# Second expert layer: slots of two and three full tiles, the rest of the first round moved into the second

## The chip, the cores and the metric

One core of one Trainium2 chip runs the whole program in one launch. The metric is device time in microseconds (us). The kernel before takes 890.9 us (median of 3 runs, 889.74 to 891.76).

## The reference

Three stages run after one another on 2304 tokens of 512 numbers, all in float32. Attention with random features (4 batches, 8 heads, 576 positions) makes `x`. A dense gated layer follows: `silu(x @ w_gate) * (x @ w_val) @ w_out` with 1536 hidden columns. Last comes a layer of 8 experts with 1024 hidden columns, in which each token goes to one expert:

```
logits = x @ w_gate + modality_bias[modality_id]
e_idx = np.argmax(logits, axis=1)
...
for e in range(E):
    mask = e_idx == e
    h = np.maximum(x[mask] @ w1[e], 0.0)
    out[mask] = gate_w[mask, None] * (h @ w2[e])
```

With the inputs of the reference only two experts are used: 1127 tokens go to expert 4 and 1177 to expert 5. Of the first 1920 tokens (15 tiles of 128) they get 934 and 986, of the last 384 tokens 193 and 191.

## The kernel before, in words

Products are made exact enough for float32 by splitting each operand into a high and a low part and adding three matmuls (`mm3`, L167 to L170). The 18 token tiles form 6 groups of 3 (`GT`). `moe1_group` (L912) runs the dense layer of a group: 12 blocks of hidden columns, each with 24 matmuls of 384 columns (into `gv`) and 9 of 512 (into `acc`). `finish` (L959) copies the three rows of results out, stores them to a scratch array in DRAM (`scr`), and schedules the logits: 24 dot products on VectorE (`logits_rows`, L735), then the softmax and the running rank of each token within its expert (`group_route`, L762).

The expert layer works in slots. A slot is 256 tokens of one expert: it loads that expert's weights (4 MB, 8 loads `raw`, L1027), splits them into 16 tiles `w` (`sp`, one copy on ScalarE and one subtraction on VectorE each, L173 and L174), gathers its token rows by an indirect DMA of GpSimd (`grow`, L1043), transposes them (`gx`, L1055; `sx`, L1057 and L1058), and runs for each of 8 blocks 12 matmuls of 256 columns (`h`) and 6 of 512 (`acc`). Between them ScalarE makes `uh` (L1094) and VectorE `ul` (L1095). The results are scaled (`orow`, L1116 and L1118) and scattered to `out` (L1120). There are two rounds: 8 slots for the first 15 tiles and 2 for the last 3. Further slots run only if a count on the chip asks for them (`more`). 

`finish_route` (L802) decides for each round, wholly on VectorE but for some small matmuls, which token goes to which slot. It is a list of pieces: `a` counts tokens, `b` builds comparisons of 15 or 3 tiles with all columns of all possible slots, then for three tiles at a time `f` makes three matrices `f_lh` and `g` multiplies with them on TensorE (`inv`, L887), and `d` reads indices out. The first round's pieces run during the last group of the dense layer, the second's during the slots.

The order on every engine is written out at build time (`manual_schedule`). `Tasks` keeps a list of pieces with due times in a planner's time: TensorE's work calls `T.step(dt)`, which first emits every piece that is due. So the planner's time fixes only the order in which each engine's queue gets its instructions; each engine then takes its own queue strictly in that order and waits by semaphores. `slot_prefetch` (L1012) places the next slot's loads, splits, gather and transposes in this way, `LQ` and `LS` the logits' dot products, `FO` and `FC` the pieces of `finish_route`:

```
fr = after + 6
T.at(T.now + fr + (FO * i if i < 2 else 2.6 * FO + FC * (i - 2)), f)
```

## Time and profile before

| | |
|---|---|
| profiled execution | 892.92 us, of which span 891.2 us |
| median of the runs | 890.9 us |
| TensorE matmul (PE) | 864.9 us busy, 97% |
| VectorE (DVE) | 616.8 us, 69% |
| ScalarE (ACT) | 390.4 us, 44% |
| GpSimd (POOL) | 92.5 us, 10% |
| mean granted TensorE clock | 0.992 of full |

The span runs from the first to the last instruction; 1.7 us of the execution lie around it. A busy share is a mean over stages with different limits: the dense layer's last group runs from about 564 to 643 us, the ten slots from there to 879 us. A matmul's listed duration overlaps the next one, so what one costs is the distance from its start to the next start.

### The profile page before, as it was taken

What the parts mean: (1) busy time and instruction counts of PE and PEld (TensorE: products, weight loads), DVE (VectorE), ACT (ScalarE), POOL (GpSimd) and SP (SyncE); (2) the same over time, 40 slices, a digit from 0 to 9 for tenths busy, and PEclk for the clock granted to TensorE, in tenths of its full rate; (3) what the DMA queues carried; (4) which work ended last, traced back from release to release, by engine and by line L of the source; (5) the groups of instructions that cost most, each with busy time, mean ns of one, the idle gap of its engine ahead of it and who ended that gap; (6) DMA issues with size and microseconds to landing.
All of it is one profiled execution on the core that took longest, in us unless ns stands there. A gap on an engine that the chain in (4) does not pass through costs nothing.

```text
span 891.2 us, 15112 instructions
## 1 busy us (share of the span) xinstructions
PE 864.9 (97%) x5320; PEld 798.7 (90%) x5320; DVE 616.8 (69%) x1565; ACT 390.4 (44%) x1071; POOL 92.5 (10%) x215
## 2 busy tenths in 40 slices
PE   7989899999999999999999999999999999999994
PEld 6879888999999999999999999999999999999993
DVE  5989899466665666566665665488777778866640
ACT  4865666343333343233344321212555555555530
POOL 6701211000000000000000000000211111111100
PEclk9989999999999999999999999999999999999998
DMA  8726542022222112131112111224497776677500
GB/s 263 209 65 202 177 162 78 8 76 54 65 54 72 36 43 54 42 95 42 42 37 60 37 26 35 57 73 175 133 337 246 245 247 228 199 233 220 174 18 22
DMA packets 91728, 103.44 MB, mean 116 GB/s; under 512 B 53600, under 2 KB 55666, under 8 KB 91643
## 3 DMA queue, kind: packets, MB, share of 16 engines
q1 hardware_dynamic: 88171, 92.35, 33.9%
q0 software_dynamic: 3200, 9.97, 3.2%
q8 instruction: 44, 0.72, 0.3%
q14 instruction: 41, 0.34, 0.1%
q10 hardware_dynamic: 272, 0.07, 0.0%
HBM read 92.91 MB, written 9.98 MB: 115 GB/s over the span
## 4 chain that ended last, share of the span: by engine, by line
PE 63%; issue 17%; DVE 7%; DMA 5%; POOL 4%; ACT 2%; POOLq 0%; DVEq 0%; ACTq 0%
PE gv L168 11%; PE gv L170 10%; PE gv L169 10%; PE acc L168 6%; PE acc L170 6%; PE acc L169 6%; DMA out_dram<-orow,sidx 5%; PE num L601 2%; PE kv L568 2%; POOL grow L1043 2%; PE qt L592 1%; PE pr L168 1%; PE xt L483 1%; PE pr L169 1%; PE pr L170 1%
## 5 line engine op out<-in xcount | busy, mean ns | idle before, releaser
L168 PE MATMUL gv<-xT,w 128*128 128x384 f32 x576 | 202.4, 351 | 1.1 <-DVE th L935 1.0
L170 PE MATMUL gv<-xT,w 128*128 128x384 f32 x576 | 194.5, 338 | 0.0
L169 PE MATMUL gv<-xT,w 128*128 128x384 f32 x576 | 194.4, 337 | 0.0
L168 PE MATMUL acc<-w,uh 128*128 128x512 f32 x360 | 146.7, 407 | 0.0
L169 PE MATMUL acc<-w,uh 128*128 128x512 f32 x360 | 141.8, 394 | 0.0
L170 PE MATMUL acc<-w,ul 128*128 128x512 f32 x360 | 141.4, 393 | 0.0
L546 ACT ACTIVATE h<-pr,mx 128x128 f32<-128x128 f32 x224 | 64.0, 369 | 138.9 <-DVE mx L541 127.3
L168 PEld LDWEIGHTS gv<-xT,w 128*128 128x128 f32 x576 | 108.9, 189 | 5.2 <-DVE th L935 2.4
L169 PEld LDWEIGHTS gv<-xT,w 128*128 128x128 f32 x576 | 109.1, 189 | 2.6
L174 DVE TENSOR_TENSOR w<-raw,w 128x512 fp32r<-128x512 f32 x160 | 106.6, 688 | 6.2 <-ACT w L173 2.4
L170 PEld LDWEIGHTS gv<-xT,w 128*128 128x128 f32 x576 | 108.7, 189 | 0.0
L747 DVE SCALAR_TENSOR_TENSOR wge<-xrow,wge 128x512 f32<-128x512 f32 x144 | 98.7, 685 | 10.1 <-DMA wge<-wg2t 9.5
L173 ACT CAST w<-raw 128x512 fp32r<-128x512 f32 x160 | 92.8, 617 | 4.3 <-DMA raw<-in_moe_w_dram 4.3
L168 PE MATMUL h<-sx,w 128*128 128x256 f32 x320 | 91.6, 286 | 0.0
L170 PE MATMUL h<-sx,w 128*128 128x256 f32 x320 | 90.5, 283 | 0.0
L169 PE MATMUL h<-sx,w 128*128 128x256 f32 x320 | 90.4, 283 | 0.0
L170 PEld LDWEIGHTS acc<-w,ul 128*128 128x128 f32 x360 | 67.6, 188 | 15.4 <-DVE ul L1095 0.2
L168 PEld LDWEIGHTS acc<-w,uh 128*128 128x128 f32 x360 | 68.0, 189 | 7.3
L169 PEld LDWEIGHTS acc<-w,uh 128*128 128x128 f32 x360 | 68.1, 189 | 7.0
L944 ACT CAST uh<-th 128x384 fp32r<-128x384 f32 x72 | 37.5, 521 | 66.2 <-DVE th L939 66.0
L935 DVE SCALAR_TENSOR_TENSOR th<-th,gv 128x384 f32<-128x384 f32 x72 | 39.7, 551 | 38.1 <-ACT th L932 38.0
L525 DVE TENSOR_REDUCE mx<-pr 128x4 f32<-128x512 f32 x72 | 49.5, 687 | 23.2 <-PE pr L170 19.7
(194 smaller groups left out, 1432.0 us busy)
## 6 DMA issues: line engine op xcount, KB each, us to landing
raw<-in_moe_w_dram SPq DMA_DIRECT2D x80, 512.0 KB, 4.8
wge<-wg2t SPq DMA_DIRECT2D x48, 256.0 KB, 3.4
wraw<-in_moe_w_gate_dram SPq DMA_DIRECT2D x12, 512.0 KB, 4.5
wraw<-in_moe_w_val_dram SPq DMA_DIRECT2D x12, 512.0 KB, 4.8
wraw<-in_moe_w_out_dram SPq DMA_DIRECT2D x12, 512.0 KB, 4.5
scr<-xrow SPq DMA_DIRECT2D x18, 256.0 KB, 2.3
xin<-in_q_dram SPq DMA_DIRECT2D x26, 128.0 KB, 2.3
xin<-in_k_dram SPq DMA_DIRECT2D x24, 128.0 KB, 2.7
```

The source lines that it names most:

```text
L168: nc.tensor.matmul(o, lh, rh, start=start, stop=False, skip_group_check=True)
L169: nc.tensor.matmul(o, lh, rl, start=False, stop=False, skip_group_check=True)
L170: nc.tensor.matmul(o, ll, rh, start=False, stop=stop, skip_group_check=True)
L173: nc.scalar.copy(hi, src)
L174: nc.vector.tensor_tensor(out=lo, in0=src, in1=hi.bitcast(F32), op=ALU.subtract)
L525: nc.vector.tensor_reduce(out=mx, in_=pr, axis=AX.X, op=ALU.max)
L546: nc.scalar.activation(out=h[:, a, :], in_=pr[:, a, :], func=ACTF.Exp, bias=mx[:, a:a + 1])
L568: nc.tensor.matmul(kv_ps[0][:, g, :], h[:, c, :], vt[:, c, 0:D + 1], start=t == own[0] and c == 0, stop=t == own[-1], skip_group_check=True)
L601: nc.tensor.matmul(num[r:r + m, h, :], st["h"][:, h, r:r + m], kv_sb[b, j][:, h, :], start=True, stop=True)
L747: nc.vector.scalar_tensor_tensor(out=st[e][:, 1, :], in0=xrows[i], scalar=1.0, in1=st[e][:, 0, :], op0=ALU.mult, op1=ALU.mult, accum_out=L ...
L935: nc.vector.scalar_tensor_tensor(out=th[f], in0=th[f], scalar=1.0, in1=ps.pop((f, "g")), op0=ALU.add, op1=ALU.mult)
L944: nc.scalar.copy(u[f][0], th[f])
```

## The change

Both rounds now count in tiles of 128 tokens. The first round takes of each expert only full tiles, in slots of two tiles (4 of them) and three tiles (2), and lowers the ranks and counts by what it took. The second round covers all 18 tiles: it holds the last three and whatever is left of the first 15, in one slot of three tiles and one of two (run in this order), and slots that run only on demand belong to it alone. So every row is stored to both scratch arrays, except the last three. `finish_route` is cut into more and smaller pieces: eight pieces `FO` apart, then the pairs `f`, `g`, where `f` now also builds its three slices of the multiplied matrix (`mv`, in the pool `rows`). The dot products of the last group come 8.5 instead of 10.37 apart, the last group's rows lie in the pool `w`, results in `rows`. A path of `wsteps` that is never taken (`n % 99 == 98` for n under 36) is gone. The core of the diff:

```diff
-LQ = (10.37, 4.52, 0.96)
+LQ = (8.5, 4.52, 0.96)
 LATE = 6
-FO = 5.72
+FO = 1.9
...
+        for g, n2, n3 in ((0, 4, 2), (1, 1, 1)):
             r = Round()
+            r.nt = (NTILE - GT, NTILE)[g]
+            r.n2, r.n3, r.fixed = n2, n3, 2 * n2 + 3 * n3
+            r.cap = g * ((NT - E) // (2 * P) + E)
+            r.C = r.fixed + 2 * r.cap
+            r.C += r.C % 2
+            r.slots = [(2, 2 * i, i) for i in range(n2)] + [(3, 2 * n2 + 3 * i, n2 + i) for i in range(n3)]
+            r.scr = dram.tile([r.nt * P, DM], F32, name=f"scr{g}")
+            r.cum = const.tile([P, E], F32, name=f"cum{g}")
             rounds.append(r)
+        nc.vector.memset(rounds[0].cum, 0.0)
...
+            return rounds[t >= rounds[0].nt]
...
+            A, B2 = rounds
+            second = r is B2
+            C, nt = r.C, r.nt
+            ts = slice(0, nt)
+            nsl = r.n2 + r.n3 + r.cap
...
+            def sums(x, k):
...
+                nc.vector.memset(s0[:, :, 0:E], 0.0)
+                nc.vector.memset(s1[:, :, 0:E], 0.0)
+                nc.vector.tensor_copy(s0[:, :, E:], x)
+                for a, b, n in ((s0, s1, 1), (s1, s0, 2), (s0, s1, 4)):
+                    nc.vector.tensor_tensor(out=b[:, :, E:], in0=a[:, :, E:], in1=a[:, :, E - n:2 * E - n], op=ALU.add)
+                return s1[:, :, E:]
+            def count():
...
+                nc.vector.tensor_tensor(out=cmp_, in0=bc(r.cum, 2, [P, E, n]),
+                                        in1=bc(THR[:, 0:n] if second else THR[:, 1:n + 1], 1, [P, E, n]),
+                                        op=ALU.is_gt if second else ALU.is_ge)
+                nc.vector.tensor_reduce(out=tl, in_=cmp_, axis=AX.X, op=ALU.add)
...
+                nc.vector.tensor_tensor(out=cmp_[:, :, 0:n], in0=bc(tl, 2, [P, E, n]),
+                                        in1=bc(cst["iota"][:, 2:2 * n + 1:2], 1, [P, E, n]), op=ALU.is_ge)
+                nc.vector.tensor_reduce(out=h, in_=cmp_[:, :, 0:n], axis=AX.X, op=ALU.add)
...
+                nc.vector.scalar_tensor_tensor(out=ab[:, 1, :], in0=h, scalar=-2.0, in1=tl, op0=ALU.mult, op1=ALU.add)
+                nc.vector.tensor_tensor(out=ab[:, 1, :], in0=ab[:, 1, :], in1=h, op=ALU.min)
+                nc.vector.tensor_tensor(out=ab[:, 0, :], in0=h, in1=ab[:, 1, :], op=ALU.subtract)
+            def place():
...
+                st["inc"] = inc = sums(ab, 2)
...
+                nc.vector.tensor_tensor(out=pre, in0=inc, in1=ab, op=ALU.subtract)
+                for i, n in enumerate((r.n2, r.n3)):
+                    nc.vector.tensor_scalar(out=got[:, i, :], in0=pre[:, i, :], scalar1=-1.0, scalar2=float(n),
+                                            op0=ALU.mult, op1=ALU.add)
+                nc.vector.scalar_tensor_tensor(out=got, in0=got, scalar=0.0, in1=ab, op0=ALU.max, op1=ALU.min)
...
+                nc.vector.tensor_tensor(out=done, in0=got[:, 0, :], in1=got[:, 1, :], op=ALU.add)
+                nc.vector.scalar_tensor_tensor(out=done, in0=done, scalar=2.0, in1=got[:, 1, :], op0=ALU.mult, op1=ALU.add)
+            def offsets():
...
+                if second:
...
+                    nc.vector.tensor_tensor(out=rest, in0=st["nt"], in1=done, op=ALU.subtract)
+                    nc.vector.tensor_tensor(out=cmp_, in0=bc(rest, 2, [P, E, n]),
+                                            in1=bc(cst["iota"][:, 1:2 * n:2], 1, [P, E, n]), op=ALU.is_ge)
+                    nc.vector.tensor_reduce(out=dn[:, 0, :], in_=cmp_, axis=AX.X, op=ALU.add)
+                    st["dinc"] = sums(dn, 1)
...
+                    nc.vector.tensor_tensor(out=offd, in0=st["dinc"][:, 0, :], in1=dn[:, 0, :], op=ALU.subtract)
+                    nc.vector.tensor_scalar(out=offd, in0=offd, scalar1=float(2 * P), scalar2=float(P * r.fixed),
+                                            op0=ALU.mult, op1=ALU.add)
+                nc.vector.tensor_scalar(out=done, in0=done, scalar1=float(P), scalar2=None, op0=ALU.mult)
...
+                nc.vector.tensor_scalar(out=lim2, in0=got[:, 0, :], scalar1=float(2 * P), scalar2=None, op0=ALU.mult)
+                nc.vector.tensor_scalar(out=off2, in0=pre[:, 0, :], scalar1=float(2 * P), scalar2=None, op0=ALU.mult)
+                nc.vector.tensor_scalar(out=off3, in0=pre[:, 1, :], scalar1=float(3 * P), scalar2=float(2 * P * r.n2),
+                                        op0=ALU.mult, op1=ALU.add)
+                nc.vector.tensor_tensor(out=off3, in0=off3, in1=lim2, op=ALU.subtract)
+                if second:
+                    nc.vector.tensor_tensor(out=offd, in0=offd, in1=done, op=ALU.subtract)
+                    nc.vector.tensor_tensor(out=offd, in0=offd, in1=off3, op=ALU.subtract)
+                nc.vector.tensor_tensor(out=off3, in0=off3, in1=off2, op=ALU.subtract)
+            def ranks():
...
+                nc.vector.tensor_tensor(out=y, in0=rk, in1=bc(st["lim2"], 1, sh), op=ALU.is_ge)
+                nc.vector.tensor_tensor(out=y, in0=y, in1=bc(st["off3"], 1, sh), op=ALU.mult)
+                nc.vector.tensor_tensor(out=x, in0=rk, in1=bc(st["off2"], 1, sh), op=ALU.add)
+                nc.vector.tensor_tensor(out=x, in0=x, in1=y, op=ALU.add)
+            def ranks2():
...
+                nc.vector.tensor_tensor(out=y, in0=rk, in1=bc(st["done"], 1, sh), op=ALU.is_ge)
+                if second:
+                    nc.vector.tensor_tensor(out=y, in0=y, in1=bc(st["offd"], 1, sh), op=ALU.mult)
+                    nc.vector.tensor_tensor(out=x, in0=x, in1=y, op=ALU.add)
+                    nc.vector.tensor_scalar(out=y, in0=rk, scalar1=0.0, scalar2=None, op0=ALU.is_lt)
+                nc.vector.scalar_tensor_tensor(out=x, in0=y, scalar=FAR, in1=x, op0=ALU.mult, op1=ALU.add)
+                nc.vector.tensor_tensor(out=x, in0=x, in1=OH[:, ts, :], op=ALU.mult)
...
+                nc.vector.tensor_reduce(out=dest, in_=x, axis=AX.X, op=ALU.add)
+                if not second:
+                    nc.vector.tensor_tensor(out=rk, in0=rk, in1=bc(st["done"], 1, sh), op=ALU.subtract)
+                    nc.vector.tensor_tensor(out=B2.cum, in0=r.cum, in1=st["done"], op=ALU.subtract)
+            def experts():
...
+                parts = [(st["inc"][:, 0, :], r.n2), (st["inc"][:, 1, :], r.n3)]
+                if second:
+                    parts.append((st["dinc"][:, 0, :], r.cap))
+                for inc, n in parts:
+                    nc.vector.tensor_tensor(out=se[:, at:at + n, :], in0=bc(inc, 1, [P, n, E]),
+                                            in1=bc(cst["iota"][:, 0:n], 2, [P, n, E]), op=ALU.is_le)
...
                 nc.vector.tensor_reduce(out=sef, in_=se, axis=AX.X, op=ALU.add)
                 nc.vector.tensor_scalar(out=r.exp_i, in0=sef, scalar1=float(E - 1), scalar2=None, op0=ALU.min)
+                if second:
...
+                    nc.vector.tensor_copy(r.tot_i, st["dinc"][:, 0, E - 1:E])
+            def columns():
...
                 nc.vector.tensor_scalar(out=thr, in0=cst["iota"][:, 0:C + 1], scalar1=float(P), scalar2=None, op0=ALU.mult)
                 nc.vector.tensor_tensor(out=ge, in0=bc(dest, 2, [P, nt, C + 1]), in1=bc(thr, 1, [P, nt, C + 1]),
                                         op=ALU.is_ge)
...
+                nc.vector.tensor_reduce(out=st["hc"], in_=ge, axis=AX.X, op=ALU.add)
+            def columns2():
...
                 nc.vector.scalar_tensor_tensor(out=lo, in0=hc, scalar=-float(P), in1=dest, op0=ALU.mult, op1=ALU.add)
                 nc.vector.tensor_scalar(out=lo, in0=lo, scalar1=float(P), scalar2=None, op0=ALU.add)
+                st["hoh"] = hoh = ge[:, :, 0:C]
                 nc.vector.tensor_tensor(out=hoh, in0=hoh, in1=ge[:, :, 1:C + 1], op=ALU.subtract)
                 hi = gp[:, :, 0].bitcast(F32R)
                 nc.vector.tensor_copy(hi, GW[:, ts])
                 nc.vector.tensor_tensor(out=gp[:, :, 1], in0=GW[:, ts], in1=gp[:, :, 0], op=ALU.subtract)
+                st["cols"] = TOK1[:, ts], gp[:, :, 0], gp[:, :, 1]
                 st["inv"] = psum.tile([P, 3, C], F32, tag="kv", name="inv", bufs=1)
+            def c(i0):
...
+                n = GT
                 def f():
+                    mv = rows.tile([P, DM], F32R, tag="row", name="f_mv")[:, 0:n * 3 * C]
+                    mv = lh["mv"] = mv.rearrange("p (i a c) -> p i a c", a=3, c=C)
+                    for i, x in enumerate(st["cols"]):
+                        nc.vector.tensor_tensor(out=mv[:, :, i, :], in0=st["hoh"][:, i0:i0 + n, :],
+                                                in1=bc(x[:, i0:i0 + n], 2, [P, n, C]), op=ALU.mult)
+                    for i in range(i0, i0 + n):
...
                         nc.vector.tensor_scalar(out=lh[i], in0=cst["iota"], scalar1=st["lo"][:, i:i + 1],
                                                 scalar2=None, op0=ALU.is_equal)
                 def g():
+                    for i in range(i0, i0 + n):
                         nc.tensor.matmul(st["inv"].rearrange("p a c -> p (a c)"), lh[i],
+                                         lh["mv"][:, i - i0].rearrange("p a c -> p (a c)"),
                                          start=i == 0, stop=i == nt - 1)
                 return f, g
             def d():
...
                 nc.vector.tensor_copy(vv, inv[:, 0, :])
+                nc.vector.tensor_scalar(out=r.gidx, in0=vv, scalar1=-1.0, scalar2=0.0, op0=ALU.add, op1=ALU.max)
                 nc.vector.tensor_copy(r.gw, inv[:, 1, :])
                 nc.vector.tensor_tensor(out=r.gw, in0=inv[:, 2, :], in1=r.gw, op=ALU.add)
                 nc.vector.tensor_scalar(out=em, in0=vv, scalar1=0.5, scalar2=float(4 * NT), op0=ALU.is_lt,
                                         op1=ALU.mult)
+                nc.vector.scalar_tensor_tensor(out=r.sidx, in0=vv, scalar=-1.0, in1=em, op0=ALU.add, op1=ALU.add)
+            return ([count, place] + ([offsets, experts] if second else [experts, offsets])
+                    + [ranks, ranks2, columns, columns2]
+                    + [f for i in range(0, nt, GT) for f in c(i)] + [d])
...
+                    if g < NG - 1:
+                        row = rows.tile([P, DM], F32, tag="row", name="xrow")
+                    else:
+                        if i % 2 == 0:
+                            pair = wpool.tile([P, 2, DM], F32, tag="w", name="xrow")
+                        row = pair[:, i % 2, :]
                     if i == 1:
                         nc.vector.tensor_copy(row, acc[i])
                     else:
                         nc.scalar.copy(row, acc[i])
+                    for r in rounds[t >= rounds[0].nt:]:
+                        nc.sync.dma_start(out=r.scr[t * P:(t + 1) * P, :], in_=row)
...
-                        T.at(T.now + fr + (FO * i if i < 2 else 2.6 * FO + FC * (i - 2)), f)
+                        T.at(T.now + fr + (FO * i if i < 8 else 8 * FO + FC * (i - 8)), f)
...
+        def slot_prefetch(r, slot, t0, dt, tg=None):
+            nt, col, s = slot
...
-                for c in (2 * s, 2 * s + 1):
-                    row = mid[0].tile([P, DM], F32, tag="grow", name="grow", bufs=2)
+                for c in range(col, col + nt):
+                    row = mid[0].tile([P, DM], F32, tag="grow", name="grow", bufs=GT)
...
-            for i in range(2):
+            for i in range(nt):
                 T.at((tg + 4 if tg else t0 + 14) + 2 * i, tr(i))
...
-                        T.step(0.66)
+                        T.step((0.66, 0.98)[nt - 2])
...
-                    c = 2 * s + i
-                    if i == 0:
-                        st["orow"] = wpool.tile([P, 2, DM], F32, tag="w", name="orow")
-                    row = st["orow"][:, i, :]
-                    if i == 0:
+                    c = col + i
+                    row = rows.tile([P, DM], F32, tag="row", name="orow")
+                    if i != 1:
...
-        slots = [(A, s) for s in range(A.nstat)] + [(Bq, s) for s in range(Bq.nstat)]
+        slots = [(A, s) for s in A.slots] + [(Bq, s) for s in Bq.slots[::-1]]
         tf = T.now + 6.5 + E * LS[0] + LA + 6
-        st = slot_prefetch(A, 0, tf + PF, PD, tf + 2.6 * FO + FC * 11 + PG)
+        st = slot_prefetch(A, A.slots[0], tf + PF, PD, tf + 8 * FO + FC * 11 + PG)
         moe1_group(NG - 1)
         cur = pending[0]
         for i, (r, s) in enumerate(slots):
             nst = None
             if i + 1 < len(slots):
-                rr, s2 = slots[i + 1]
-                nst = slot_prefetch(rr, s2, T.now - 3.5, 1.25)
+                nst = slot_prefetch(*slots[i + 1], T.now - 3.5, (1.25, 1.9)[s[0] - 2])
...
-        over = mid_pool.tile([P, 2], F32, name="over")
-        over_i = mid_pool.tile([P, 1], I32, name="over_i")
...
+                more(s + 1, tot)
+        more(0, nc.values_load(Bq.tot_i[0:1, 0:1], min_val=0, max_val=Bq.cap))
```

## Rows read from the trace of the kernel before

**Rows 1.** Waits of all engines, 600 to 850 us: total, times, longest.
```profile
PEld acc L170 <- DVE ul L1095: 0.2, 1, 0.2
```

**Rows 2.** TensorE in time, one block of a slot: start, us, instruction.
```profile
708.25 0.28 PE L168 MATMUL h<-sx,w 128*128 128x256 f32 x1
...
709.68 0.40 PE L168 MATMUL acc<-w,uh 128*128 128x512 f32 x1
...
711.07 0.28 PE L168 MATMUL h<-sx,w 128*128 128x256 f32 x1
```

**Rows 3.** GpSimd in time: first scatter of two slots in a row.
```profile
788.35 1.02 POOL L1120 DMA_INDIRECT out_dram<-orow,sidx  x1 [10.41 <-ACT orow L1116]
...
811.79 1.02 POOL L1120 DMA_INDIRECT out_dram<-orow,sidx  x1 [10.40 <-ACT orow L1116]
```

**Rows 4.** TensorE in time, one block of the dense layer.
```profile
570.46 0.33 PE L168 MATMUL gv<-xT,w 128*128 128x384 f32 x1
...
574.64 0.39 PE L168 MATMUL acc<-w,uh 128*128 128x512 f32 x1
...
576.73 0.33 PE L168 MATMUL gv<-xT,w 128*128 128x384 f32 x1
```

**Rows 5.** TensorE in time: one group of the routing's matmuls and what follows.
```profile
768.26 0.41 PE L887 MATMUL inv<-f_mv,f_lh 128*128 128x54 f32 x3
...
768.83 0.40 PE L169 MATMUL acc<-w,uh 128*128 128x512 f32 x1
```

**Rows 6.** VectorE in time: vector instructions of the first round's routing, by size.
```profile
607.84 0.17 DVE L822 COPY f_s<-f_ns 128x8 f32<-128x8 f32 x1
608.04 0.17 DVE L823 TENSOR_TENSOR f_s<-f_s 128x8 f32<-128x8 f32 x1
...
609.38 0.28 DVE L834 TENSOR_TENSOR f_tmp<-f_tmp,OH 128x120 f32<-128x120 f32 x1
609.69 0.28 DVE L836 TENSOR_REDUCE f_dest<-f_tmp 128x15 f32<-128x120 f32 x1
...
613.77 0.65 DVE L858 TENSOR_TENSOR f_ge<-f_dest,f_thr 128x465 f32<-128x465 f32 x1
614.45 0.64 DVE L861 TENSOR_REDUCE f_hc<-f_ge 128x15 f32<-128x465 f32 x1
...
616.78 1.16 DVE L872 TENSOR_TENSOR f_mv<-f_ge,f_gp 128x450 fp32r<-128x450 f32 x2
...
622.41 0.68 DVE L882 TENSOR_SCALAR f_lh<-IOTA,f_lo 128x128 fp32r<-128x128 f32 x3
```

**Rows 7.** VectorE in time: its idle time while the first round is routed.
```profile
612.01 0.55 DVE L935 SCALAR_TENSOR_TENSOR th<-th,gv 128x384 f32<-128x384 f32 x1 [0.62 <-ACT th L932]
613.09 0.55 DVE L939 SCALAR_TENSOR_TENSOR th<-th,gv 128x384 f32<-128x384 f32 x1 [0.53 <-PE gv L170]
...
624.63 0.68 DVE L882 TENSOR_SCALAR f_lh<-IOTA,f_lo 128x128 fp32r<-128x128 f32 x3 [0.95 <-PE inv L887]
...
631.43 0.19 DVE L899 COPY f_v<-inv 128x30 f32<-128x30 f32 x1 [0.92 <-PE inv L887]
```

**Rows 8.** ScalarE in time: first split of the first slot's weights.
```profile
615.96 0.62 ACT L173 CAST w<-raw 128x512 fp32r<-128x512 f32 x1 [1.77 <-DMA raw<-in_moe_w_dram]
```

**Rows 9.** Stretches: length, then PE, PEld, DVE, ACT, POOL busy, clock, DMA share, GB/s.
```profile
785.00:808.00 23.00, 23.00 (x152) 20.97 (x151) 15.28 (x27) 12.61 (x27) 4.38 (x4) 1.00 0.69 224
```

**Rows 10.** VectorE in time, ordinary slot work, and one wait for the transposes.
```profile
729.68 0.69 DVE L1058 TENSOR_TENSOR sx<-gx,sx 128x512 fp32r<-128x512 f32 x1 [0.83 <-ACT sx L1057]
...
757.21 1.28 DVE L174 TENSOR_TENSOR w<-raw,w 128x512 fp32r<-128x512 f32 x2
758.41 0.42 DVE L1095 SCALAR_TENSOR_TENSOR ul<-h,uh 128x256 fp32r<-128x256 f32 x1
```

**Rows 11.** Stretches early in the kernel, columns as in group 9.
```profile
56.00:60.00 4.00, 2.52 (x12) 2.19 (x13) 3.15 (x9) 2.03 (x13) 0.44 (x2) 0.68 0.59 166
60.00:64.00 4.00, 4.00 (x16) 4.00 (x14) 4.00 (x8) 2.06 (x7) 0.78 (x2) 0.50 0.35 119
```

More of the change, by code (lines that the diff above doesn't have):

```diff
@@ L56 @@
 P = 128
-SLOT = 256
 class Tasks:
@@ L407, in a @@
                 st["r"] = wraw.pop(key)
[L409 to L412 removed]
+                st["t"] = rows.tile([P, DM], I32, tag="row", name="wt")
                 nc.vector.tensor_scalar(out=st["t"], in0=st["r"][:, :, 1], scalar1=3, scalar2=0x3FFFFFFF,
@@ L962, in finish @@
                     t = g * GT + i
-                    r = round_of(t)
-                    row = rows.tile([P, DM], F32, tag="row", name="xrow")
+                    if g < NG - 1:
[4 more added lines that the diff above has]
+                        row = pair[:, i % 2, :]
                     if i == 1:
@@ L1051, in f @@
                     if i == 0:
-                        st["x"] = [xpool.tile([P, KD, SLOT], F32R, tag=f"xT{a}", name=f"sx{a}") for a in range(2)]
+                        st["x"] = [xpool.tile([P, KD, nt * P], F32R, tag=f"xT{a}", name=f"sx{a}") for a in range(2)]
                     xt = misc([P, KD, P], "gx")
@@ L1097, in l1, with l2 @@
                 u[f] = (uh, ul)
-            def l2(f, half=(0, 1)):
+            def l2(f, half=range(nt)):
                 uh, ul = u[f]
@@ L1326, with more @@
         T.drain()
-        def more(r, s, tot):
-            if s == r.cap:
+        def more(s, tot):
+            if s == Bq.cap:
                 return
             with tc.If(tot > s):
-                st = slot_prefetch(r, s, T.now, 1)
+                slot = 2, Bq.fixed + 2 * s, Bq.n2 + Bq.n3 + s
+                st = slot_prefetch(Bq, slot, T.now, 1)
                 T.drain()
-                slot_body(r, s, st, None)()
+                slot_body(Bq, slot, st, None)()
                 T.drain()
-                more(r, s + 1, tot)
-        over = mid_pool.tile([P, 2], F32, name="over")
-        over_i = mid_pool.tile([P, 1], I32, name="over_i")
-        for i, r in enumerate(rounds):
-            nc.vector.tensor_scalar(out=over[:, i:i + 1], in0=r.tot_f, scalar1=-float(r.nstat), scalar2=None,
-                                    op0=ALU.add)
-        nc.vector.tensor_tensor(out=over_i, in0=over[:, 0:1], in1=over[:, 1:2], op=ALU.max)
-        ov = nc.values_load(over_i[0:1, 0:1], min_val=-16, max_val=16)
-        with tc.If(ov > 0):
-            for r in rounds:
-                more(r, r.nstat, nc.values_load(r.tot_i[0:1, 0:1], min_val=0, max_val=r.cap))
+                more(s + 1, tot)
+        more(0, nc.values_load(Bq.tot_i[0:1, 0:1], min_val=0, max_val=Bq.cap))
 _INS = ['q', 'k', 'v', 'omega', 'moe_w_gate', 'moe_w_val', 'moe_w_out', 'moe2_modality_id', 'moe2_w_gate',
```

169 lines of the change are left out of this document (63 added, 106 removed).

## The prediction

> **What bounds the kernel now.** The page's busy shares come first: TensorE 97%, VectorE 69%, so a gain must shorten TensorE's queue, and a loss appears where that queue is made to wait. The view of waits for the dense layer's last group and the slots holds one wait of a TensorE queue on data, 0.2 us [rows 1]. TensorE's own order in time then prices a slot. One block is 12 matmuls of 256 columns in 1.43 us and 6 of 512 in 1.39 [rows 2]; 8 blocks make 22.56 us. Two slots' scatters lie 23.44 us apart [rows 3], which leaves 0.88 us for two transposes, 0.44 each. Wide shapes come from the dense layer: 24 matmuls of 384 columns take 4.18 us, 9 of 512 take 2.09 [rows 4]. Last I read VectorE in time, since the change adds most instructions there.
>
> **The slots.** Before, ten slots of two tiles take 234.4 us. After, the inputs fill the new slots exactly. Expert 4 (934 tokens in the first 15 tiles) and expert 5 (986) give 7 full tiles each, two pairs and a triple apiece, which are the 4 and 2 slots of the first round. There remain 934 - 896 + 193 = 231 and 986 - 896 + 191 = 281 tokens, two and three tiles, which are the second round's two slots; no slot on demand runs. So 5 slots of two tiles and 3 of three remain, 19 tiles for 20. A triple is 8 × (2.09 + 2.09) + 3 × 0.44 = 34.76 us. New sum: 5 × 23.44 + 3 × 34.76 = 221.5 us, **-12.9 us**. Narrow matmuls are dearer per column (1.43/12/256 = 0.47 ns against 4.18/24/384 = 0.45), and one tile is gone. The last slot still has two tiles, so its tail is as before; the small `over` count after it goes, at most 0.3 us, taken as nothing.
>
> The Trainium skill (TensorE: Matmul & The Clock Gate, section "Wait — 56ns, not 53.3ns?") puts matmuls at the full clock at N/2.4 GHz plus about 2.5 ns from start to start: 109, 163 and 216 ns for 256, 384 and 512 columns. The rows have 119, 174 and 232 ns, so the trace doesn't agree, and it decides; by the page the slots' term would be an estimated -11.2 us.
>
> **More routing matmuls.** Three `inv` matmuls move the following work from 768.26 to 768.83, of which one 512-column step is 0.23: 0.34 us a group [rows 5]. The second round has six groups instead of one, **+1.7 us**. The first round keeps its five; they get narrower (42 columns for 90), which I take as nothing (between -0.3 and 0).
>
> **VectorE's price list.** A small instruction that needs the last one's result starts 0.20 us after it; one of 120 elements 0.31; one of 465 elements 0.68; two independent ones of 450 take 1.16, so 0.54 from start to start against 0.62 of one alone; three `f_lh` take 0.68, 0.20 each [rows 6]. Between them about 1 ns an element.
>
> **First round's routing.** Old `a` has 9 small instructions and 5 of 120 elements, `b` 5 small and 6 of about 450, then 15 `f_lh` and 6 to read out: some 3.5 + 4.3 + 3.0 + 0.9 = 11.7 us. New: count 1.75 (four of 120 or 56, three small), place 1.95 (ten small), experts 0.7, offsets 0.85, ranks 2.85 (ten of 120), columns 2.05 (three of about 220), five groups of three `mv` (0.12) and three `f_lh`, 4.8, read out 0.9: 15.9 us. That is 4.2 us more in nearly the same planner's time (the read-out is due 21.2 after the first piece, was 20.9). VectorE's idle time there, 3.0 us, is what could hide it; 1.9 of that are waits for `inv` itself [rows 7], which come late when VectorE does. Also, the expert numbers that the weight loads wait for were the first piece's result and are now the third's, due 3.8 later; ScalarE already waited 1.77 us for the first load [rows 8], and behind that copy queue the dense layer's `th` and, on VectorE, the whole rest. I take TensorE to stand **+3.0 us** at `inv`: 4.2, plus 1.3 of later load, less 2.5 of idle time. Bounds 0.5 (all idle time usable, load hidden) and 5.
>
> **Second round's routing.** It grows from 3 tiles × 18 columns to 18 × 38. Pieces: count 1.8, place 1.95, offsets 3.0 (sixteen small), experts 1.15, ranks 3.3 (eleven of 144), columns 2.1 and 1.4 (three of about 700, 0.9 each), six groups of three `mv` of 114 elements (0.19) and three `f_lh`, 6.9, read out 0.9: 22.5 us, against about 6 before. They are due over 15.2 + 12 × 0.6 = 22.4 of planner's time, from 78 after the last group's `finish`: the end of the fourth slot and two thirds of the fifth, the first triple. In us TensorE needs 22.4 × 1.07 (a block planned at 4 × 0.65 takes 2.82 us) + 3 transposes + six `inv` groups, about 27 us. The ordinary vector work emitted in between: twelve splits at 0.60 [rows 10], seven `ul` at 0.34 to 0.47, three `sx`, one `orow`: 12.8 us. So VectorE has 35.3 us for TensorE's 27, 8.3 short. Each `sx` waits for ScalarE behind the transpose, 0.83 us at worst [rows 10], which can't be filled in a strict queue: about 2 us more. Just before this stretch stands the last group's softmax, a row of small instructions, so the lag that `ul` can bear is already used; I count 0.7 for it. Behind a late piece stand `ul`, which the block's second matmuls need, and `f_lh`, which TensorE's next instruction needs. I take TensorE's standstill as **+11 us** (8.3 + 2 + 0.7). Lower bound 0: an ordinary slot leaves VectorE idle for 7.7 of 23 us [rows 9] and `ul` has some slack, so all might be swallowed. Upper bound 15.5: 22.5 less that idle share of 27 us, 9.0, plus the 2.
>
> Hidden at no cost: the 15 second stores of rows (SyncE and the DMA queues are idle in the dense layer, and the rows wait for their dot products far longer); a third gather per triple, about 1 us of GpSimd, which is busy 4.4 of 23 us [rows 9]; results in `rows`, whose three buffers have a slot's time to leave. If a gather came late, TensorE would stand at `gx`.
>
> **Sum.** -12.9 + 1.7 + 3.0 + 11 = +2.8 us on the profiled execution's 892.9, so 895.7. That execution is 2.0 us above the median, so the forecast is **893.7 us**. A measurement of this kernel can tell about 0.2%, 1.8 us, from no change.
>
> **Rivals.**
> 1. *The vector work is hidden* (faster). Place: `ul` and `f_lh` in the fifth slot. Price: none as long as VectorE's lag stays under the time between a block's first and second matmuls, about 2 us in a pair and 3 in a triple. For it: the old routing blocks of 3 to 4 us passed with no wait of TensorE [rows 1]. Against it: they were single blocks, these follow one another every 2 us. Standstills of 2 us in all would give -12.9 + 1.7 + 2 = -9.2: 881.7 us.
> 2. *Half hidden.* If splits of the next slot can be late without harm and the standstill is 7 us in both places: -4.2, 886.7 us.
> 3. *The clock falls too* (slower still). Where TensorE stood for 1.5 of 4 us early in the kernel, the granted clock went to 0.68 and then 0.50, the 1.2 GHz level, for the next 4 us [rows 11]. A wait of several us at the first `inv` could do this once or twice; at half speed 4 us of work take 8. Since VectorE is the bound just there, I count 4 us in all: 897.7 us. The Trainium skill's section "What's actually happening" on the same page says that an idle array is given half the pulses; by it this would occur after each long wait. The trace agrees with the fall, and shows in these rows what it costs.
> 4. *The layout doesn't fit* and slots on demand run: at least 23 us more. The counts of tokens above speak against it.
>
> **Chances.** Forecast 0.53 (its own range 889.5 to 897: the two standstills together 10 to 17 us), rival 1 0.14, rival 2 0.18, rival 3 0.14, rival 4 0.01. Faster by over 0.2% (below 889.1): rivals 1 and 2, 0.32. Within 0.2%: the forecast's lower part, 0.22. Slower: its upper part with rivals 3 and 4, 0.46. The range 884 to 898.5 leaves out rival 1's best cases and the rarest of 3 and 4.
>
> **What would show it.** Right: triples some 34.8 us apart where nothing waits; TensorE idle at `inv` with `f_lh` as releaser in both rounds; VectorE at full load from the fourth slot's end through two thirds of the fifth, which lasts some 45 us; the first weight load about 1.5 us later. Wrong: no idle time of TensorE in the fifth slot (rival 1), or a granted clock of 0.5 in it (rival 3), or more than eight slots (rival 4).

## The result, and the profile after

The changed kernel takes 897.24 us (median of 5 runs, 895.30 to 898.37) against 890.9: a ratio of 1.0066 (95% interval 1.0047 to 1.0086), 6.3 us slower, where 2.8 us slower was forecast (893.7 us). Its profiled execution took 898.11 us, with a span of 896.4 against 891.2 before: 5.2 us of difference, since the execution profiled before lay 2.0 us above its median and this one 0.9.

The page, its head and the row of the clock:

```profile
span 896.4 us, 14599 instructions
...
PE 860.2 (96%) x5115; PEld 790.7 (88%) x5115; DVE 606.5 (68%) x1610; ACT 370.5 (41%) x1023; POOL 93.3 (10%) x213
...
PEclk9999999999999999999999999999999999899998
```

TensorE is still the bound overall, but the clock's row has a new 8 in the 35th slice (762 to 784 us). TensorE's waits of 600 to 850 us (engine, line, what was waited for; us in all, times, longest) answer to [rows 1], where there was one of 0.2:

```profile
PE inv L969 <- DVE f_lh L964: 7.8, 5, 3.7
PE acc L166 <- DVE orow L1206: 1.0, 1, 1.0
PE acc L168 <- DVE ul L1185: 0.8, 1, 0.8
PE gx L1143 <- DVE sx L1146: 0.3, 1, 0.3
```

All of them end on VectorE. One of the five at `inv`, 1.25 us, lies in the first round (627.48), the other four, 6.5 us, in the second. The first matmuls of the fifth to eighth slot in TensorE's order show where they lie:

```profile
742.41 0.33 PE L166 MATMUL h<-sx,w 128*128 128x384 f32 x1
...
791.60 0.33 PE L166 MATMUL h<-sx,w 128*128 128x384 f32 x1
...
826.43 0.33 PE L166 MATMUL h<-sx,w 128*128 128x384 f32 x1
...
860.81 0.28 PE L166 MATMUL h<-sx,w 128*128 128x256 f32 x1
```

The sixth slot, a triple in which nothing waits, takes 34.83 us (34.76 forecast). The fifth, a triple too, takes 49.19; without a wait some 36.2 would be due: 34.83, less 0.70 because the slot before it is a pair (6 matmuls of 512 columns of that slot's last block run in it, not 9), and six `inv` groups of 0.34. Its middle by stretches of 4 us (length, then busy PE, PEld, DVE, ACT, POOL, the granted clock, DMA share, GB/s; as in [rows 9]):

```profile
748.00:752.00 4.00, 2.16 (x9) 1.16 (x9) 3.86 (x14) 2.04 (x4) 0.12 (x1) 1.00 0.17 66
752.00:756.00 4.00, 4.00 (x22) 3.65 (x21) 3.76 (x13) 1.00 (x2) 0.88 (x1) 1.00 0.19 70
756.00:760.00 4.00, 3.31 (x20) 2.81 (x18) 3.90 (x10) 1.60 (x3) 0.00 (x0) 1.00 0.44 143
760.00:764.00 4.00, 0.97 (x8) 0.95 (x8) 3.97 (x13) 0.00 (x0) 0.00 (x0) 1.00 0.66 250
764.00:768.00 4.00, 2.96 (x10) 2.04 (x9) 3.57 (x14) 1.10 (x2) 0.00 (x0) 0.54 0.00 0
768.00:772.00 4.00, 4.00 (x17) 3.47 (x16) 1.01 (x4) 1.10 (x2) 0.00 (x0) 0.61 0.23 38
772.00:776.00 4.00, 2.91 (x15) 2.07 (x13) 2.56 (x11) 1.20 (x3) 0.00 (x0) 1.00 0.24 93
```

Read the two halves apart. Up to 764 VectorE is busy 15.5 of 16 us and TensorE 10.4: VectorE is the bound. From 764 to 772 the clock is at 0.54 and 0.61, TensorE works through almost all of it at about half speed, and now VectorE has time left (1.01 of 4 us). The whole stretch from the first to the last of the second round's routing instructions, in the same columns:

```profile
740.18:780.27 40.09, 31.70 (x154) 26.76 (x153) 33.37 (x129) 11.36 (x22) 2.02 (x2) 0.91 0.32 109
```

Of VectorE's 33.37 us, 21.7 are the routing's own instructions (22.5 forecast).

TensorE's longest wait, in its order (a wait costs more than the idle time listed: the matmul before this one starts at 758.97, 4.06 us earlier, where a step between such matmuls is 0.17):

```profile
763.03 0.71 PE L969 MATMUL inv<-f_mv,f_lh 128*128 128x114 f32 x3 [3.72 <-DVE f_lh L964]
```

For the first round, VectorE in time (answers to [rows 6, 7]) and ScalarE's first split ([rows 8]):

```profile
608.97 0.28 DVE L823 TENSOR_TENSOR f_cmp<-cum,THR 128x120 f32<-128x120 f32 x1
...
613.44 0.17 DVE L922 TENSOR_SCALAR exp_i<-f_sef 128x6 int32<-128x6 f32 x1
...
635.44 0.17 DVE L982 TENSOR_SCALAR gidx<-f_v 128x14 int32<-128x14 f32 x1
```

```profile
618.53 0.62 ACT L171 CAST w<-raw 128x512 fp32r<-128x512 f32 x1 [2.66 <-DMA raw<-in_moe_w_dram]
```

From the first routing instruction to `gidx` 26.47 us pass (24.52 before), and TensorE stands for 1.25 us at the first `inv`.

One thing was not foreseen. The copy of a dense group's first row, before and then after:

```profile
278.11 0.59 ACT L968 COPY xrow<-acc 128x512 f32<-128x512 f32 x1
379.51 0.59 ACT L968 COPY xrow<-acc 128x512 f32<-128x512 f32 x1
```

```profile
278.99 0.59 ACT L1055 COPY xrow<-acc 128x512 f32<-128x512 f32 x1
380.82 0.59 ACT L1055 COPY xrow<-acc 128x512 f32<-128x512 f32 x1
```

A group takes 101.40 us before and 101.83 after, in a part of the kernel whose matmuls the change doesn't touch.

### The profile page after: what moved, and what is told of

Same layout as the page of the kernel before. It is cut to its first block, busy times and chain, and to the rows that moved or that the text cites. A ratio compares the mean times of both kernels' runs of the same rounds, so it can differ in the third digit from the quotient of the medians.

```text
span 896.4 us, 14599 instructions
## 1 busy us (share of the span) xinstructions
PE 860.2 (96%) x5115; PEld 790.7 (88%) x5115; DVE 606.5 (68%) x1610; ACT 370.5 (41%) x1023; POOL 93.3 (10%) x213
## 5 line engine op out<-in xcount | busy, mean ns | idle before, releaser
L166 PE MATMUL acc<-w,uh 128*128 128x512 f32 x352 | 144.3, 410 | 1.0 <-DVE orow L1206 1.0
L167 PE MATMUL acc<-w,uh 128*128 128x512 f32 x352 | 139.3, 396 | 0.0
L172 DVE TENSOR_TENSOR w<-raw,w 128x512 fp32r<-128x512 f32 x128 | 85.8, 687 | 6.4 <-ACT w L171 5.5
L166 PE MATMUL h<-sx,w 128*128 128x256 f32 (+1 forms) x256 | 78.4, 306 | 0.0
L168 PE MATMUL h<-sx,w 128*128 128x256 f32 (+1 forms) x256 | 77.6, 303 | 0.0
L167 PE MATMUL h<-sx,w 128*128 128x256 f32 (+1 forms) x256 | 77.5, 303 | 0.0
L171 ACT CAST w<-raw 128x512 fp32r<-128x512 f32 x128 | 74.4, 617 | 5.9 <-DMA raw<-in_moe_w_dram 5.9
L166 PEld LDWEIGHTS acc<-w,uh 128*128 128x128 f32 x352 | 66.7, 189 | 8.6 <-DVE orow L1206 1.5
L167 PEld LDWEIGHTS acc<-w,uh 128*128 128x128 f32 x352 | 66.8, 190 | 7.3
```

Of the source, the lines that this page charges most:

```text
L166: nc.tensor.matmul(o, lh, rh, start=start, stop=False, skip_group_check=True)
L167: nc.tensor.matmul(o, lh, rl, start=False, stop=False, skip_group_check=True)
L168: nc.tensor.matmul(o, ll, rh, start=False, stop=stop, skip_group_check=True)
L171: nc.scalar.copy(hi, src)
L172: nc.vector.tensor_tensor(out=lo, in0=src, in1=hi.bitcast(F32), op=ALU.subtract)
```

## The experiments

Twelve kernels. The theory (density): the second round's vector work stands too densely for the TensorE time beside it. Rivals: the hand-off at `inv` itself (each group's vector part stands directly ahead of its matmuls); the clock; the second stores.

**e1_spread: the second round's pieces farther apart.**

```diff
+FO2 = 2.6
+FC2 = 1.0
...
-                        T.at(T.now + fr + (FO * i if i < 8 else 8 * FO + FC * (i - 8)), f)
+                        fo, fc = (FO2, FC2) if g == NG - 1 else (FO, FC)
+                        T.at(T.now + fr + (fo * i if i < 8 else 8 * fo + fc * (i - 8)), f)
```

> The second round's routing pieces alone are due farther apart (2.6 and 1.0 of planner's time instead of 1.9 and 0.6, so 32.8 in all instead of 22.4); the work is the same. Theory (density: VectorE has more to do than TensorE's time between the pieces holds): the fifth slot, 49.2 us in the changed kernel, takes 40 to 43 us, the granted clock stays at 1.00 in it, and the time is 6 to 9 us below the changed kernel's 897.2: 888 to 891 us. Rival (handshake: each of the six inv groups waits for vector instructions that are only begun when the one before is done): the six waits stay as they are, slot 48 to 50 us, time 896 to 898 us.

887.32 us, ratio to before 0.9964 (0.9950 to 0.9978): with two constants the slower kernel is faster than the one before. The fifth slot takes 39.67 us (39.86 in e5_address below, which has the same second round: so closely two executions agree). TensorE's waits from 600 to 850 us:

```profile
PE inv L971 <- DVE f_lh L966: 2.9, 3, 1.4
PE acc L168 <- DVE orow L1209: 1.0, 1, 1.0
PE gx L1146 <- DVE sx L1149: 0.3, 1, 0.3
```

Of the three at `inv` one, 1.36 us, is the first round's. The clock stays at 1.00, though TensorE stood for 1.4 us here too:

```profile
764.00:768.00 4.00, 2.62 (x16) 2.58 (x16) 4.00 (x16) 0.00 (x0) 0.00 (x0) 1.00 0.14 55
768.00:772.00 4.00, 4.00 (x24) 3.62 (x23) 3.27 (x15) 1.52 (x3) 0.00 (x0) 1.00 0.04 4
```

Density holds, and by a little more than it promised (40 to 43 us, 888 to 891).

**e2_lag: each `inv` group's vector part one piece ahead, in both rounds.**

```diff
-                    mv = rows.tile([P, DM], F32R, tag="row", name="f_mv")[:, 0:n * 3 * C]
...
+                    mt = rows.tile([P, DM], F32R, tag="row", name="f_mv")
...
-                        lh[i] = t_("f_lh", [P, P], F32R, bufs=GT)
+                        lh[i] = mt[:, DM - P:DM] if i == i0 else t_("f_lh", [P, P], F32R, bufs=2 * GT - 2)
...
+            cs = [c(i) for i in range(0, nt, GT)]
...
+                seq = [cs[0][0]] + [f for x, y in zip(cs, cs[1:]) for f in (y[0], x[1])] + [cs[-1][1]]
```

> In both rounds the vector part of each inv group is put one piece earlier, ahead of the matmuls of the group before, so that no inv matmul follows its own vector part at once; the number of instructions and the due times of the first and last piece are as in the changed kernel. Handshake theory: all waits at inv but the first go (3.6 us in the second round's triple and most of what follows from them), 888 to 891 us. Density theory: the first wait of 3.7 us stays, the others move in part to ul, 2 to 4 us are won, 893 to 895 us, and the clock still falls after the first wait.

890.57 us, 0.9993 (0.9983 to 1.0004). The fifth slot takes 44.49 us, 4.7 less than in the changed kernel.

```profile
PE inv L969 <- DVE f_mv L964: 3.9, 3, 3.3
PE acc L166 <- DVE orow L1209: 1.0, 1, 1.0
PE acc L168 <- DVE ul L1188: 0.8, 1, 0.8
```

The time lies in the rival's range, the picture is the theory's: the first wait stays (3.3 us), the clock falls after it (0.81 and 0.76 in 760 to 768), and the later waits at `inv` are gone. So the hand-off was a part of the loss, some 4.7 of 13 us, and not the first cause. The parts overlap: due times spread wider, with this order as it was, take the same waits away (e9_spread_wide).

**e7_narrow: less vector work, same due times.**

```diff
-            r.cap = g * ((NT - E) // (2 * P) + E)
+            r.cap = g
```

> The changed kernel with room for one slot on demand instead of sixteen in the second round's layout: 8 columns instead of 38, with all pieces and their due times as they are (none of the slots on demand is reached with these inputs). By the price list of about 1 ns an element VectorE has some 4.5 us less to do (three instructions of 700 elements become three of 150, eighteen mv of 114 become 24). Density theory: the standstill shrinks by about as much, 4 to 6 us, the triple takes 43 to 45 us, time 891 to 893 us. Rival (handshake: the chain of waits at inv, whatever the width): at most 1 us less, 896 to 897 us.

890.73 us, 0.9994 (0.9985 to 1.0004). The routing's vector instructions are 3.8 us shorter (17.9 for 21.7; 4.5 expected). The fifth slot takes 46.20 us, 3.0 less, short of the 4 to 6 forecast; the clock fell here as well (0.61 and 0.54 in 760 to 768), with no wait longer than 1.7 us:

```profile
PE inv L969 <- DVE f_lh L964: 5.2, 5, 1.7
```

The width counts, so it isn't the chain of hand-offs alone. The other 3.3 us of the gain lie where nobody expected them, behind the last scatter: from its start to the end of the span the changed kernel takes 9.5 us (886.92 to 896.4), this one 6.2 (883.94 to 890.1). The nest of slots on demand is one level deep here and not sixteen, the only thing that the edit changes there; the other kernels with sixteen levels take 9.4 to 9.5 us.

**e9_spread_wide: only the due times, farther still.**

```diff
-LQ = (8.5, 4.52, 0.96)
+LQ = (6, 4.52, 0.96)
...
+FO2 = 4.5
+FC2 = 1.4
```

`FO2` and `FC2` are used as in e1_spread.

> Of e6_all only the due times: the second round's logits 6 an expert, its pieces 4.5 and 1.4 apart; the inv groups and the places in SBUF as in the changed kernel. Density theory: the fifth slot takes 36.5 to 37.5 us against 39.7 in e1_spread and 36.1 in e6_all, the clock stays at 1.00; with the dense groups at 101.85 us and the first round's wait of 1.3 us as in the changed kernel the time is 880.8 + 1.6 + 0.6 + up to 1 = 883 to 884 us. Rival (e6_all's gain over e1_spread came from the inv order): slot of 38.5 us or more, 885 us or more.

885.06 us, 0.9927 (0.9910 to 0.9943). The fifth slot takes 37.37 us, in the range; no wait of TensorE is listed in it.

```profile
741.00 0.33 PE L168 MATMUL h<-sx,w 128*128 128x384 f32 x1
...
778.37 0.33 PE L168 MATMUL h<-sx,w 128*128 128x384 f32 x1
```

The time is 1 us above the range and just in the rival's (885 us or more), but the rival's slot of 38.5 us or more did not come. The first slot is 0.4 us longer than in e6_all, and the start of the slots 2.5 us later, not 2.2. Of the 13.05 us between the changed kernel's fifth slot and e6_all's, the due times alone bring back 11.8.

**e6_all: all of it.** The edits of e9_spread_wide, e2_lag and e5_address (below) together.

> All remedies together: the second round's logits are due sooner (6 instead of 8.5 an expert), its pieces farther apart (4.5 and 1.4), the vector part of an inv group one piece ahead in both rounds, and the old places in SBUF. Density theory: the triple that holds the second round's routing loses nearly all of its standstill, 36.5 to 37.5 us instead of 49.2 (34.8 and six inv groups of 0.34 make 36.9), the clock stays at 1.00, and the time is 883 to 885 us. Rival (the dot products, now 24 in 48 instead of 68 of planner's time, delay the splits of the slots before): slots 1 to 4 grow by 1 us or more each and the time is 887 or more.

880.82 us, ratio to before 0.9885 (0.9869 to 0.9902): 10.3 us faster than the kernel before and 16.4 faster than the changed one, with the same 14,599 instructions. It is 2 us below the expected range: the triple with the routing takes 36.14 us, 0.4 less than the lowest value named, and the slots start at 642.78, 3.6 us sooner than in the changed kernel, more than the 0.6 and 1.5 counted for the first round and the places. Of these, 1.8 lie ahead of the first dense group's copy, where executions of the same instructions differ by up to 3 us (table below): chance. The rival fell, since the first four slots take 95.33 us together, 95.99 in the changed kernel. TensorE's only waits (both in the first round), the first matmuls of the fifth to seventh slot, the busiest stretch of the routing, and all of it from its first to its last vector instruction:

```profile
PE inv L969 <- DVE f_mv L964: 0.6, 2, 0.4
```

```profile
738.11 0.33 PE L168 MATMUL h<-sx,w 128*128 128x384 f32 x1
...
774.25 0.33 PE L168 MATMUL h<-sx,w 128*128 128x384 f32 x1
...
809.05 0.33 PE L168 MATMUL h<-sx,w 128*128 128x384 f32 x1
```

```profile
756.00:760.00 4.00, 4.00 (x24) 3.69 (x24) 3.82 (x15) 2.29 (x5) 0.00 (x0) 1.00 0.47 135
```

```profile
712.96:774.76 61.80, 61.80 (x361) 56.24 (x360) 53.16 (x165) 29.51 (x59) 8.20 (x7) 1.00 0.55 182
```

In its busiest stretch VectorE is as full as before the standstill of the changed kernel (3.82 of 4 us), and TensorE is too. The same routing work, 21.8 us, lies in 61.8 us and not in 40.1.

**e4_fill and e10_fill_more: the clock by itself.** Matmuls that nobody reads stand where TensorE waited, so that it is kept at work. e10_fill_more:

```diff
+FILL = {0: 36, 3: 12, 9: 8, 12: 12}
...
                 def g():
+                    if second and i0 in FILL:
+                        fill = misc([P, 2 * P], "fill")
+                        for _ in range(FILL[i0]):
+                            nc.tensor.matmul(fill, om_h[:, 0:P], om_h, start=True, stop=True)
```

e4_fill has the same with 24 matmuls ahead of the first group (`i0 == 0`) alone.

> 24 matmuls of 256 columns that nobody reads (2.9 us at the full clock) stand ahead of the second round's first inv, where TensorE waited for 3.7 us. Theory (the clock's fall after that wait costs some 3 us): the granted clock stays at 1.00 in the fifth slot, which takes 46 to 47 us instead of 49.2, and the time is 893.5 to 895.5 us. Rival (VectorE sets the pace there, so the slow clock costs nothing): 896.5 to 898 us with the clock at 1.00. If the wait weren't there the 24 would add 2.9 us: 900 us.

895.12 us, 1.0048 (1.0031 to 1.0065), fifth slot 48.29. The clock still fell, later and less far:

```profile
764.00:768.00 4.00, 3.63 (x15) 3.08 (x16) 2.46 (x11) 0.05 (x1) 0.00 (x0) 0.72 0.00 0
768.00:772.00 4.00, 3.88 (x20) 3.51 (x20) 2.44 (x8) 1.12 (x3) 0.00 (x0) 0.85 0.47 131
```

The time pointed to the theory, the clock's row didn't; hence the second one.

> The changed kernel with 36, 12, 8 and 12 matmuls that nobody reads (8.1 us at the full clock) ahead of the second round's first, second, fourth and fifth inv group, where TensorE stood for 8.4 us in all between 748 and 780; e4_fill's 24 delayed the fall of the clock and did not stop it. Theory (the slow clock costs 2.9 us): the clock stays at 1.00, the fifth slot takes 46 to 47 us instead of 49.2, time 893 to 895 us. Rival (VectorE sets the pace, the slow clock costs nothing): slot of 49 us, 896 to 898 us; where the matmuls don't fit into the waits it gets longer still.

896.15 us, 1.0052 (1.0035 to 1.0069), fifth slot 47.60. Now the clock holds:

```profile
764.00:768.00 4.00, 3.97 (x24) 3.40 (x23) 3.39 (x15) 1.10 (x2) 0.00 (x0) 1.00 0.00 0
768.00:772.00 4.00, 4.00 (x29) 3.87 (x28) 2.65 (x10) 1.11 (x2) 0.00 (x0) 1.00 0.40 131
```

The slot is 1.6 us shorter than the changed kernel's, between the two expectations, and TensorE no longer waits at the second round's `inv`, so some of the 68 matmuls stood in its way. By this one pair of executions the fall of the clock cost at least 1.6 us; the rows bound it at 2.9 (TensorE's busy time at the lower clock, 2.96 × 0.46 + 4.00 × 0.39). The totals of the changed kernel and these two overlap in their intervals; only the slot's length tells them apart, and e3_one_store, whose second round is the changed kernel's, has a slot of 49.76.

How far the clock falls differs between executions. At the first round's first `inv`, where e4_fill has the changed kernel's instructions, the changed kernel waited 1.25 us and e4_fill 1.41 us; the changed kernel first, then e4_fill:

```profile
624.00:628.00 4.00, 2.75 (x16) 2.41 (x15) 3.93 (x16) 2.86 (x6) 0.00 (x0) 1.00 1.06 398
```

```profile
624.00:628.00 4.00, 3.67 (x15) 3.38 (x16) 4.00 (x20) 0.99 (x3) 0.00 (x0) 0.73 0.78 288
```

So one trace each of e4_fill and e10_fill_more is thin evidence for how many matmuls hold the clock.

**e3_one_store: rows stored once.**

```diff
-            r.scr = dram.tile([r.nt * P, DM], F32, name=f"scr{g}")
+            r.scr = rounds[0].scr if g else dram.tile([NT, DM], F32, name="scr")
...
-                    for r in rounds[t >= rounds[0].nt:]:
-                        nc.sync.dma_start(out=r.scr[t * P:(t + 1) * P, :], in_=row)
+                    for t2 in (t, t + GT)[:1 + (g == NG - 2)]:
+                        nc.sync.dma_start(out=rounds[0].scr[t2 * P:(t2 + 1) * P, :], in_=row)
...
```

> Both rounds gather from one array of all 18 tiles, so a row of the first 15 tiles is stored once and not twice (three rows more are stored in the fifth group as a filling). Theory: the 12 second stores make the dense groups 0.4 us longer each; then the first split copy of a row of group 4 is again where it was before the change, 562.4 us against 564.0, and the time 1.5 us lower, 895 to 896.5 us. Rival: the 1.6 us are what one execution differs from another; then it stands anywhere from 562 to 564.5 and the time is 896 to 898 us. A store of the last group that must wait for a gather out of the same array could cost up to 2 us more.

897.81 us, 1.0073 (1.0054 to 1.0093); a group from copy to copy 101.87 and 101.84 us. The theory fell: the second stores cost nothing, as forecast, and the longer groups were no accident of one execution: all variants with the changed layout show them.

**e5_address, e8_before_moved, e11_before_moved_128: the same instructions, other places.** The table `THR` grew from 8 to 19 numbers a partition. By the order of allocation all buffers behind the constants then lie 64 bytes higher.

```diff
-        REV = const.tile([P, E], F32, name="REV")
-        THR = const.tile([P, NTILE + 1], F32, name="THR")
+        REV = const.tile([P, 2 * E], F32, name="REV")[:, 0:E]
...
+        cst["thr"] = mid_pool.tile([P, NTILE + 1], F32, name="THR")
...
```

That is e5_address, on e1_spread: the constants have their old size again. The other two are the kernel before with a larger one (24, and 40 in e11_before_moved_128):

```diff
-        THR = const.tile([P, 8], F32, name="THR")
+        THR = const.tile([P, 24], F32, name="THR")[:, 0:8]
```

> The kernel of e1_spread with the table THR moved out of the constants, so that all later buffers in SBUF lie where they lay before the change (64 bytes lower than after it). Same instructions. Theory (the operands' place): the matmuls of the projection pr, from start to start 0.114 us before and 0.118 after, are 0.114 again, a dense group takes 101.4 us from one row's copy to the next group's instead of 101.85, and the time is 1.3 to 1.7 us below e1_spread's 887.3: 885.6 to 886.0 us. Rival (the 0.43 us a group come from the second stores or from something else in the change): groups of 101.85 us and 887 to 888 us.

> The kernel before with 64 unused bytes a partition in the constants, which put all later buffers where the changed kernel has them. Theory (the operands' place): dense groups of 101.85 us instead of 101.4, pr matmuls 0.118 instead of 0.114, time 1.3 to 1.7 us above before: 892.3 to 892.9 us. Rival (the place doesn't matter): no difference, 890.9 to 891.5 us, groups of 101.4.

> The kernel before with 128 unused bytes a partition in the constants instead of e8_before_moved's 64. If the place modulo 128 bytes decides, the pr matmuls are 0.114 us from start to start again and a dense group takes 101.4 us; if it matters where the buffers lie otherwise, 0.118 and 101.85 as with 64, or something else.

The projection's matmuls in 180 to 480 us, grouped (duration min/median/max in ns): before, after, e5_address, e8_before_moved, e11_before_moved_128.

```profile
L168 PE MATMUL pr<-om_h,xh x70: 275/276/283, 186.7 to 475.3; 128*128 128x256 f32 x70
```

```profile
L166 PE MATMUL pr<-om_h,xh x70: 279/281/287, 187.1 to 476.9; 128*128 128x256 f32 x70
```

```profile
L168 PE MATMUL pr<-om_h,xh x70: 275/276/283, 184.9 to 473.7; 128*128 128x256 f32 x70
```

```profile
L168 PE MATMUL pr<-om_h,xh x70: 279/281/287, 183.3 to 473.0; 128*128 128x256 f32 x70
```

```profile
L168 PE MATMUL pr<-om_h,xh x70: 276/279/282, 185.0 to 474.5; 128*128 128x256 f32 x70
```

Same place, same duration, in both directions. The first two groups take 101.41 and 101.55 us in e5_address, 101.88 and 101.83 in e8_before_moved, 101.67 and 101.80 with 128 bytes, so it isn't the place modulo 128 alone. Of the 0.9 us that two groups differ before and after, from start to start, the 144 matmuls of the projection make 0.65 and the 576 of `gv` 0.25. In whole times e8_before_moved is 892.88 us, 1.0021 (1.0011 to 1.0032) of before. e5_address is 886.93 (0.9942 to 0.9975), only 0.4 below e1_spread, within both intervals: there the gain stands in the trace alone. e11_before_moved_128 ran once, 891.91.

**e12_first_round: the first round's pieces farther apart too** (e6_all with `FO = 2.1`).

> e6_all with the first round's eight vector pieces 2.1 instead of 1.9 of planner's time apart, so that its inv groups come 1.6 later and the gather with them. Density theory: the two waits at the first round's inv in e6_all, 0.6 us, go, and the time is 0.3 to 0.6 us lower, which can hardly be told: 880.2 to 880.6 us. Rival: the later gather makes TensorE wait at the first transposes, or the first split copies come later; 881 us or more.

881.09 us, 0.9891 (0.9874 to 0.9907), no difference from e6_all. The waits at `inv` went, as the theory says, and the rival's came:

```profile
PE gx L1147 <- DMA grow<-scr,gidx: 0.5, 1, 0.5
PE h L169 <- DVE sx L1150: 0.3, 1, 0.3
```

## Why the forecast came out so: its steps

The forecast was 893.7 us, and its own range 889.5 to 897; 897.24 lies just above that and next to rival 3's 897.7, and the sign named for rival 3 came: a granted clock of about 0.5 in the fifth slot. So the slots and the place of the standstill were foreseen, and the outcome is the forecast's mechanism with rival 3's on top. That the total is so near to rival 3's is in part luck: it counted 4 us for the clock, where 1.6 to 2.9 are seen, and terms that were not foreseen make up the rest.

The difference of the two profiled executions, cut at marks in the trace (the last group before the second layer, the first `h`, the last matmul, the end):

| step | forecast | measured | how |
|---|---|---|---|
| eight slots for ten, with the `inv` groups | -12.9 + 1.7 = -11.2 | -11.0 | first `h` to last matmul, 224.96 us in e6_all (nearly no wait) against 235.96 before |
| second round's standstill | +11 | +13.7 | the same stretch, 238.68 in the changed kernel |
| first round's standstill | +3.0 | +1.85 | fifth group's ranks to first `h`, 81.85 against 80.00 |
| buffers moved | not seen | +1.2 | first group's copy to the fifth group's ranks, 387.45 against 386.22 |
| up to the first group's copy | - | +0.4 | 177.12 against 176.69: chance, since the kernels with the changed places have the same instructions up to here and take 173.95 (e4_fill) to 177.12 us |
| behind the last matmul | 0 | -1.0 | 11.30 against 12.33 us to the end |
| sum | +2.8 | +5.2 | spans 896.4 and 891.2 (medians: +6.3) |

**The slots** were right, and the rows were the right price. By the Trainium skill's spacing (TensorE: Matmul & The Clock Gate, section "Wait — 56ns, not 53.3ns?") the first line would be an estimated -9.5; e6_all has -11.0.

**The second round** was the right mechanism with the right place, and mis-sized. The fifth slot took 49 us where some 45 were named. The forecast counted VectorE's work and the `sx` hand-offs, but took rival 3 for a case of its own, when it came with the standstill: 3.7 us without a matmul, then 0.54 and 0.61. That is 1.6 to 2.9 us, about what was missing (2.7). The section "What's actually happening" of the same page of the Trainium skill says an idle array is given half the pulses. The trace agrees after this wait; after e1_spread's of 1.4 us the clock stayed at 1.00. The forecast's other half, that VectorE simply lacks 8.3 us there, holds for the due times given alone: e6_all does the same work, begun sooner, and its slot takes 36.14 us, what a triple behind a pair takes with six `inv` groups and no wait.

**The first round** was mis-sized the other way. The term was 4.2 us of vector work and 1.3 of later load, less 2.5 of idle time. The vector work was counted too high: the round's routing instructions keep VectorE busy for 14.55 us against 11.59, 3.0 more and not 4.2. The load did come later, by 1.1 us (`exp_i` at 613.44 against 610.64, less the 1.66 by which all of this stretch starts later), and ScalarE's wait for it grew by 0.9. The whole way to the read-out grew by 1.95 (26.47 against 24.52). How much each of the two adds to TensorE's 1.85 no run here separates.

**Not in the forecast at all** was the table's size moving every other buffer (+1.2 us), or that the program's end gets shorter by more than the 0.3 us that were taken as nothing. The errors of the terms partly cancel: 2.7, 1.2 and 0.4 us too little, 1.15 and 1.0 too much. The second stores were rightly put at nothing, though not because the DMA queues are idle in the dense layer: their share of busy time from 200 to 560 us was 0.19 before.

Rivals 1 and 2 fell: the two standstills are 15.6 us together, not 2 or 7. Rival 3 came, at a lower price. Rival 4 fell, since eight slots run. Of the signs named, the triples 34.83 apart, TensorE idle at `inv` behind `f_lh` in both rounds, a full VectorE in the fifth slot and a first load 1.1 us later (1.5 named) came.

## What to carry to other kernels

Where work moves from one engine's slack into another's stream, its due times decide as much as its amount: spread the pieces over the whole time until their result is needed, before judging the change; here the same number of instructions cost 13.7 us or next to nothing, and in the slot that holds them due times alone brought back 11.8 of 13.05 us. A standstill of TensorE must be priced with the lower clock that can follow it. And when a kernel gets slower in a part that wasn't edited, compare the durations of single instruction groups and the places of their operands before looking for contention.

## What the runs showed of the hardware

- The projection's matmuls of 256 columns take 276 ns, and 281 when all buffers behind the constants lie 64 bytes higher in SBUF (279 with 128 bytes): most of 1.2 us over the dense groups, in both directions. By the order of allocation the moving operand `om_h` lies at the same place in all these kernels, and the stationary ones, `xh` and `xl`, have moved, but so have other buffers in use at the time. Which of them counts, and which property of the place, stays open.
- After 3.7 us without a matmul the granted clock was 0.54 and 0.61 for two stretches of 4 us; TensorE kept at work with unread matmuls stayed at 1.00. It also fell with no single wait above 1.7 us (e7_narrow), where TensorE had been busy 2.43, 4.00 and 2.98 of 4 us, and around a wait of 1.41 us in e4_fill (0.73), where the changed kernel stayed at 1.00 with 1.25 us.
- A nest of sixteen levels of branches that are not taken, instead of one, lengthened the end of the program by 3.3 us (9.5 against 6.2 us from the last scatter's start). What takes this time isn't shown.
